# A low-rank product transposed on three row tiles instead of one, with its second operand loaded three times

## The chip, the cores and the metric

The kernel runs on one core of a Trainium2 chip. The metric is the device time of one execution in microseconds (us); lower is better. Engines are named as in the profile: PE is TensorE (PEld its weight loads), DVE is VectorE, ACT is ScalarE, POOL is GpSimd, SP is SyncE. DMA transfers are issued by SP and ACT ("hardware" queues) or by POOL ("software" queue) and carried out by 16 DMA engines of the core.

## What is computed

`x` is 8 x 4224 x 192 in float32. A causal convolution along the 4224 positions, with 7 taps and one set of softmax weights for each of 8 heads of 24 channels, gives y. Then a mixer follows:

```
xt = y.transpose(0, 2, 1)
h  = xt @ U @ V                      # U: 4224 x 32, V: 32 x 4224
u  = y + h.transpose(0, 2, 1)
out = u + np.maximum(u @ w_ch1, 0.0) @ w_ch2    # 192 -> 768 -> 192
```

So for each batch there is a small 32 x 192 product tt = U^T y over all positions, and h at a position is the matching column of V times tt.

## The kernel before, in words

**Tiles and groups.** The 8 x 4224 positions are cut into 264 tiles of 128 positions (33 for each batch), and 8 tiles make a group; there are 33 groups, `g` = 0 to 32. In a group the 8 tiles are numbered by a half `hf` (0 or 1) and `i` (0 to 3). The 192 channels are three blocks `c` of 64.

**Stages of a group.** `conv` or `conv32` make y of a batch as matmuls with banded matrices, `tt_mm`, `tt_split` and `tt_sum` make tt of a batch. `h_group` (L457 matmul, L479 addition on DVE) makes u, and `transp` (L498) transposes u by a DMA of SP's queue into `uT`, with positions along the columns and 64 channels of each half on 64 partitions. `w1` (L554 matmul, L568 and L570 ReLU on ACT and DVE) is the first layer from uT, `w2` (L583 matmul, L592 addition on DVE, L600 store) the second layer. The order is written out by hand: SLOTS lists which groups' first and second layers come when, and what lies between them. Every engine runs its own instructions in program order; semaphores make it wait for others.

**Groups 0 and 1 are special.** To start the first layer early, their u is not made first and then transposed. `yT_part` (L509) transposes y into PSUM by matmuls with the identity matrix, and `hT_part` (L524) adds the transposed h to the same PSUM bank: it multiplies 64 columns (block c) of tt with a stretch of V. ACT and DVE then copy the bank into `uT` (L256, L258 within `evac`). tt of batch 0 (`ttb[0]`, a tile of 128 partitions) is made with the matrix R4, which sums the four parts of 32 partitions and writes the sum four times, so that all four blocks of 32 partitions hold the same tt. `V0_sb` holds the first 2048 columns of V for these two groups. The rows of V and tt are 32, so a matmul of hT_part uses 32 of PE's 128 rows; `tile_position` names the row and the column at which it lies. The two halves hf lie on columns 0 and 64.

**Order at the start on PE:** convolution of batch 0 in pieces, tt (L402, L741, and L682 for the last piece, which reads `U4_sb`), yT_part(0), hT_part(0) with 10 matmuls, the rest of yT_part(1), hT_part(1) with 6 matmuls, w1(0), h_group(2), w1(1).

**POOL's order at the start:** x of batch 0 (two loads), U (two), x of batch 0 (two more), V0_sb (L133), W1_sb in four pieces (L137), zeroing and first piece of x of batch 1 (L74, L79), a copy that makes U4_sb (L701), V_sb in four quarters and a rest (L715, L722; read by L457 from h_group(2) on), W2_sb (L726), three more pieces of x of batch 1 (L79), copies for band2 (L759), and then x of the next batch. POOL's loads take turns on eight semaphores, so that one waits until the eighth before it has landed.

The lines of hT_part that the change touches are these:

```
lhsT=ttb[0][0:R, HB * c : HB * c + HB],
rhs=V0_sb[:, t0 + i0 * P : t0 + i1 * P],
tile_position=(0, HB * hf),
```

with R = 32, HB = 64 and P = 128.

Of the kernel before, what the change touches and what calls it, by code (L numbers as in the profile page):

```python
# [9 lines left out]
BF16 = mybir.dt.bfloat16  # L10
# [4 lines left out]
def kernel(  # L15
# [10 lines left out]
    nc = tc.nc  # L26
    P = nc.NUM_PARTITIONS
# [3 lines left out]
    R = moe_U.shape[1]  # L31
# [4 lines left out]
    GT = 8  # L36
# [3 lines left out]
    HB = P // 2  # L40
# [4 lines left out]
    cst = ctx.enter_context(tc.tile_pool(name="cst", bufs=1))  # L45
# [57 lines left out]
    def iota(t, pattern, base, mul):  # L103
# [20 lines left out]
        out=Ur[:, 0:nfull, :], in_=U4[0 : nfull * P, :].rearrange("(k p) c -> p k c", p=P)  # L124
# [4 lines left out]
        x_piece(k)  # L129


    V0_sb = cst.tile([R, 2 * GT * P], BF16, name="V0_sb")
    nc.gpsimd.dma_start(out=V0_sb[:], in_=moe_V[:, 0 : 2 * GT * P])  # L133
    W1_sb = cst.tile([P, 3, M4], BF16, name="W1_sb")
    for m0, m1 in ((0, 2 * P), (2 * P, M4)):
        for hf in range(2):
            nc.gpsimd.dma_start(  # L137
                out=W1_sb[HB * hf : HB * hf + HB, :, m0:m1],
                in_=moe_w_ch1[:, m0:m1].rearrange("(c k) m -> k c m", k=HB),
# [27 lines left out]
    for hh in range(2):  # L167
# [3 lines left out]
        out=dif[:], in0=dif[:], scalar1=rq[:, 0:1], scalar2=None, op0=ALU.add  # L171
# [5 lines left out]
        out=d_sb[:],  # L177
# [8 lines left out]
        out=hot[:],  # L186
# [6 lines left out]
        out=ident[:], in0=fp[:], scalar1=float(P), scalar2=None, op0=ALU.is_equal  # L193
# [9 lines left out]
        out=c_sb[:].rearrange("p k h -> p h k"),  # L203
# [5 lines left out]
    for hh in range(2):  # L209
# [3 lines left out]
            out=pr[:],  # L213
# [8 lines left out]
        out=Eq[:], in0=efp[:], scalar1=rq[:, 1:2], scalar2=None, op0=ALU.is_equal  # L222
# [3 lines left out]
        out=fp[:], in0=fp[:], scalar1=R - 1, scalar2=None, op0=ALU.bitwise_and  # L226
# [3 lines left out]
        out=R4[:], in0=fp[:], scalar1=0.0, scalar2=None, op0=ALU.is_equal  # L230
# [23 lines left out]
    def evac(eng, out, in_):  # L254
        if eng == "A":
            nc.scalar.activation(out=out, in_=in_, func=ACT.Copy)  # L256
        else:
            nc.vector.tensor_copy(out=out, in_=in_)  # L258
# [135 lines left out]
    ttb = [[] for _ in range(B)]  # L394
# [123 lines left out]
    def hT_part(g, parts):  # L518

        uTt[g] = uts.tile([P, 4, 3, P], BF16, name="uT")  # L520
        for c, i0, i1, p, _ in parts:
            for hf in range(2):
                t0 = (2 * g + hf) * 4 * P
                nc.tensor.matmul(  # L524
                    out=p[HB * hf : HB * hf + HB, 0 : (i1 - i0) * P],
                    lhsT=ttb[0][0:R, HB * c : HB * c + HB],
                    rhs=V0_sb[:, t0 + i0 * P : t0 + i1 * P],
                    start=False,
                    stop=True,
                    tile_position=(0, HB * hf),  # L530
                )
        for c, i0, i1, p, eng in parts:
            evac(
                eng,
                uTt[g][:, i0:i1, c, :],
                p[:, 0 : (i1 - i0) * P].rearrange("p (i t) -> p i t", t=P),
            )
# [161 lines left out]
    for r, (k0, k1) in KP[2].items():  # L699
        j = NB0 // 2 * r + k0  # L700
        nc.gpsimd.tensor_copy(  # L701
            out=U4_sb[:, o : o + k1 - k0, :, :],
            in_=U_sb[:]
# [9 lines left out]
    for q in range(4):  # L713
        src = moe_V[:, 0 : full * 8 * P].rearrange("r (k q t) -> r k q t", q=4, t=2 * P)
        nc.gpsimd.dma_start(  # L715
            out=V_sb[32 * q : 32 * q + 32, 0 : 2 * full, :].rearrange(
                "r (k a) t -> r k (a t)", a=2
            ),
            in_=src[:, :, q, :],
# [3 lines left out]
        out=V_sb[0:32, 2 * (NT // 8), :], in_=moe_V[:, (NT - 1) * P : NT * P]  # L723
# [23 lines left out]
    yT_part(1, parts1)  # L747
    tt_done(0, ps0)
    hT_part(0, parts0 + more)
    rest = [(c, 0, 4, bank(), "ADA"[c]) for c in (1, 2)]  # L750
    yT_part(1, rest)
    hT_part(1, parts1 + rest)
    band2 = cst.tile([P, H, QB], BF16, name="band2")
    for xp in XP[1:]:
        x_part(1, *xp)
    for r in range(4):
        q = slice(QB * r, QB * r + QB)
        for hh in range(2):
            nc.gpsimd.tensor_copy(  # L759
                out=band2[q, HQ * hh : HQ * hh + HQ, :],  # L760
                in_=bands[hh][q, :, HB * (r % 2) : HB * (r % 2) + QB],
# [86 lines left out]
```

## Time and profile before

| | |
|---|---|
| time, median of 3 runs | 324.98 us (324.97 to 325.1) |
| span of the profiled execution, first to last instruction | 323.2 us |
| PE busy | 317.6 us (98%) |
| DVE, ACT, POOL busy | 268.6, 170.0, 142.7 us |
| granted clock of PE | 1.000 |
| L524 (hT_part) | 16 matmuls, 18.34 to 20.5 us |
| L133 (V0_sb) | 1 load of 128 KB, issued at 7.23 us, landed 7.9 us later |
| L715 (V_sb) | 4 loads of 64 KB, issued from 14.04 us on |

For the profiled execution the page gives the span; the runs' time is 1.8 us above it, and no other time of that execution is given. Times within the profile are counted from the span's start. Busy time of PE includes matmuls that lie side by side once only, and the end of each is modelled. A load's landing is counted from the start of its issue on POOL.

### The profile page before, as it was taken

To read this page: it belongs to the slowest core of one execution; us is meant where nothing else is said; L and a number is where in the kernel's file an instruction comes from. 1 tells how busy PE (TensorE), PEld (TensorE's weight loads), DVE (VectorE), ACT (ScalarE), POOL (GpSimd) and SP (SyncE) were. 2 spreads that over 40 slices of the span, in tenths; PEclk is the share of its full clock that TensorE was granted. 3 is DMA by queue.
4 is the path that set the end of the run, shared out by engine and by line. 5 is a ranking of instruction groups with operands and counts; after the bars stand their busy time and mean duration, and the time that the engine had idled before them with its cause. 6 is when DMAs were issued, how large, how long until landed. Compare 5 with 4: busy or idle time off the path is not lost.

```text
span 323.2 us, 9583 instructions
## 1 busy us (share of the span) xinstructions
PE 317.6 (98%) x3996; PEld 223.7 (69%) x3996; DVE 268.6 (83%) x551; ACT 170.0 (53%) x344; POOL 142.7 (44%) x111
## 2 busy tenths in 40 slices
PE   8999999999999999999999999999999999999995
PEld 3747676478677647866864884687797497487495
DVE  6769989987977986997898699789888897896863
ACT  1766724860874397088239609824903902912910
POOL 8764179728957983992897497000000000000000
PEclk9999999999999999999999999999999999999999
DMA  9999993999998999599499957138268059048035
GB/s 106 192 191 183 206 209 100 196 192 257 208 135 200 246 142 190 166 189 209 130 237 192 181 149 194 52 105 231 61 178 262 3 150 275 18 121 271 2 121 173
DMA packets 122906, 53.51 MB, mean 166 GB/s; under 512 B 87760, under 2 KB 122832, under 8 KB 122864
## 3 DMA queue, kind: packets, MB, share of 16 engines
q1 hardware_dynamic: 84528, 38.08, 45.4%
q0 software_dynamic: 38192, 14.73, 39.2%
q8 instruction: 31, 0.51, 0.7%
q10 hardware_dynamic: 144, 0.10, 0.1%
q14 instruction: 11, 0.09, 0.1%
HBM read 29.49 MB, written 25.95 MB: 172 GB/s over the span
## 4 chain that ended last, share of the span: by engine, by line
PE 92%; ACT 3%; DMA 2%; DVE 1%; issue 0%; POOL 0%; POOLq 0%
PE ps L583 42%; PE ps L554 39%; PE ps L339 3%; PE ps L457 3%; DMA x_sb<-in_x_dram 2%; PE ps L402 2%; ACT rl_sb L568 2%; PE ps L369 1%; ACT y_sb L256 1%; PE ps L509 1%; DVE u_sb L479 1%; DVE rl_sb L570 1%; PE ps L524 0%; PE ps L428 0%; POOL x_sb L79 0%
## 5 line engine op out<-in xcount | busy, mean ns | idle before, releaser
L568 ACT ACTIVATE rl_sb<-ps 128x512 bf16<-128x512 f32 x233 | 124.3, 604 | 108.0 <-PE ps L554 96.0
L583 PE MATMUL ps<-W_sb,rl_sb 128*128 128x192 bf16 x1584 | 141.2, 246 | 0.2
L583 PEld LDWEIGHTS <-rl_sb 128*128 128x128 bf16 x1584 | 128.3, 98 | 11.8 <-issue 11.5
L554 PE MATMUL ps<-uT,W_sb 64*128 64x512 bf16 x1188 | 131.7, 376 | 0.0
L570 DVE TENSOR_SCALAR rl_sb<-ps 128x512 bf16<-128x512 f32 x163 | 105.3, 688 | 15.7 <-PE ps L554 15.4
L554 PEld LDWEIGHTS <-W_sb 64*128 64x128 bf16 x1188 | 66.9, 94 | 60.4 <-issue 3.9
L592 DVE TENSOR_TENSOR out_sb<-ps,u_sb 128x384 f32<-128x384 f32 (+1 forms) x133 | 70.4, 551 | 25.5 <-PE ps L583 25.0
L305 POOL COPY xb_sb<-x_sb 32x3072 bf16<-32x3072 bf16 (+1 forms) x24 | 67.4, 2824 | 0.5
L479 DVE TENSOR_TENSOR u_sb<-y_sb,ps 128x192 bf16<-128x192 bf16 (+1 forms) x168 | 66.3, 461 | 0.0
L293 POOL COPY xb_sb<-x_sb 128x3072 bf16<-128x3072 bf16 x12 | 32.7, 2742 | 42.1 <-PE ps L339 32.2
L256 ACT ACTIVATE y_sb<-ps 128x384 bf16<-128x384 f32 (+4 forms) x90 | 38.3, 520 | 9.7 <-PE ps L339 7.4
L79 POOL DMA_DIRECT2D x_sb<-in_x_dram x32 | 27.0, 848 | 9.6 <-PE ps L457 3.8
L258 DVE CAST y_sb<-ps 128x408 bf16<-128x408 f32 (+4 forms) x36 | 19.1, 578 | 1.3 <-PE ps L369 1.0
L457 PE MATMUL ps<-tt_sb,V_sb 32*128 32x192 bf16 x264 | 12.4, 246 | 0.1
L339 PE MATMUL ps<-x_sb,band 64*32 64x384 bf16 x192 | 12.1, 333 | 0.0
L339 PE MATMUL ps<-xb_sb,band 64*32 64x384 bf16 x192 | 12.1, 332 | 0.0
L457 PEld LDWEIGHTS <-V_sb 32*128 32x128 bf16 x264 | 4.7, 92 | 7.3 <-issue 7.3
L416 ACT ACTIVATE tt_hi<-ps 128x192 bf16<-128x192 f32 x8 | 2.6, 330 | 11.9 <-PE ps L402 11.9
L369 PE MATMUL ps<-x_sb,band 64*64 64x240 bf16 (+3 forms) x192 | 8.0, 276 | 0.2 <-DMA x_sb<-in_x_dram 0.2
L339 PEld LDWEIGHTS <-band 64*32 64x32 bf16 x384 | 4.5, 89 | 5.2 <-issue 2.4
L153 PE MATMUL ps<-zz 128*128 128x512 f32 (+1 forms) x10 | 6.7, 816 | 1.1 <-DVE zz L143 1.1
L369 PEld LDWEIGHTS <-band 64*64 64x64 bf16 x192 | 6.0, 106 | 2.1 <-issue 1.4
(65 smaller groups left out, 71.3 us busy)
## 6 DMA issues: line engine op xcount, KB each, us to landing
out_dram<-out_sb SPq DMA_DIRECT2D x131, 192.0 KB, 2.7
x_sb<-in_x_dram POOLq DMA_DIRECT2D x14, 384.0 KB, 6.9
x_sb<-in_x_dram POOLq DMA_DIRECT2D x7, 432.0 KB, 6.7
x_sb<-in_x_dram POOLq DMA_DIRECT2D x7, 408.0 KB, 8.0
x_sb<-in_x_dram POOLq DMA_DIRECT2D x1, 504.0 KB, 7.3
uT<-u_sb SPq DMA_TRANSPOSE x31, 3.5
x_sb<-in_x_dram POOLq DMA_DIRECT2D x1, 480.0 KB, 5.6
W_sb<-in_moe_w_ch_dram POOLq DMA_DIRECT2D x2, 192.0 KB, 7.8
```

Source lines behind the costliest of these rows:

```text
L79: return nc.gpsimd.dma_start(out=xt[b][HB * r : HB * r + HB, s0:s1, :], in_=x[b, blk * HB : (blk + s1 - s0) * HB, :].rearrange("(j p) d -> ...
L256: nc.scalar.activation(out=out, in_=in_, func=ACT.Copy)
L293: nc.gpsimd.tensor_copy(out=xbt[b][:, s0:s1, :], in_=xt[b][:, s0 + 1 : s1 + 1, :])
L305: nc.gpsimd.tensor_copy(out=xbt[b][q, s0:s1, :], in_=xt[b][q, s0:s1, :])
L339: nc.tensor.matmul(out=pp[r][QB * cg : QB * cg + QB, 0 : nk[r] * GS], lhsT=w[hr], rhs=t[hr, st : st + 2 * nk[r] - 1 : 2, hs], start=True, ...
L457: nc.tensor.matmul(out=banks[pr][:, a * D : (a + 1) * D], lhsT=V_sb[32 * q : 32 * q + 32, (j // 8) * 2 + j % 2, :], rhs=ttb[b][32 * q : 32 ...
L479: nc.vector.tensor_tensor(out=u_group(g)[:, i : i + n, :, hf, :], in0=yt[b][:, run[0] : run[0] + n, :].rearrange("p n (c k) -> p n c k", c=3),
L554: last = nc.tensor.matmul(out=pps[m][hf][:], lhsT=W1_sb[HB * hf : HB * hf + HB, c, m * P : (m + 1) * P], rhs=uTt[g][HB * hf : HB * hf + HB ...
L568: nc.scalar.activation(out=rl[:, m, hf, :], in_=pp[hf][:], func=ACT.Relu)
L570: nc.vector.tensor_scalar_max(out=rl[:, m, hf, :], in0=pp[hf][:], scalar1=0.0)
L583: last = nc.tensor.matmul(out=cps[:, a * D : (a + 1) * D], lhsT=rlt[g][:, m, hf, (i + a) * P : (i + a + 1) * P], rhs=W2_sb[:, m, :], start ...
L592: nc.vector.tensor_tensor(out=o[:, 0:n, :].rearrange("p n (c k) -> p n c k", c=3), in0=cps[:, 0 : n * D].rearrange("p (n c k) -> p n c k", ...
```

## The change

V0_sb gets 96 partitions instead of 32, and the same part of V is loaded three times by POOL, to partitions 0, 32 and 64. In hT_part, block c of the channels uses the rows 32c to 32c + 31 of tt's tile and of V0_sb, and the matmul lies on those rows of PE. The numbers, sizes and order of the matmuls stay as they are. On POOL's queue there are two more loads, ahead of W1's; what follows waits for landings that lie two loads further on. Line numbers from L134 on move by one.

```diff
-    V0_sb = cst.tile([R, 2 * GT * P], BF16, name="V0_sb")
-    nc.gpsimd.dma_start(out=V0_sb[:], in_=moe_V[:, 0 : 2 * GT * P])
+    V0_sb = cst.tile([3 * R, 2 * GT * P], BF16, name="V0_sb")
+    for c in range(3):
+        nc.gpsimd.dma_start(out=V0_sb[R * c : R * c + R, :], in_=moe_V[:, 0 : 2 * GT * P])
...
-                    lhsT=ttb[0][0:R, HB * c : HB * c + HB],
-                    rhs=V0_sb[:, t0 + i0 * P : t0 + i1 * P],
+                    lhsT=ttb[0][R * c : R * c + R, HB * c : HB * c + HB],
+                    rhs=V0_sb[R * c : R * c + R, t0 + i0 * P : t0 + i1 * P],
...
-                    tile_position=(0, HB * hf),
+                    tile_position=(R * c, HB * hf),
```

## The prediction

> **What bounds the kernel now.** I read the page first: busy times and the chain that ended last.
>
> ```profile
> PE 317.6 (98%) x3996; PEld 223.7 (69%) x3996; DVE 268.6 (83%) x551; ACT 170.0 (53%) x344; POOL 142.7 (44%) x111
> PE 92%; ACT 3%; DMA 2%; DVE 1%; issue 0%; POOL 0%; POOLq 0%
> ```
>
> The end is set by TensorE (PE) nearly everywhere, so time that PE saves is kept unless a wait takes it back. Second, the chain in order of time, from the stage that the change touches to the first layer of group 1:
>
> ```profile
> 17.89 0.46 PE ps L509 x12
> 18.35 0.83 PE ps L524 x10
> 19.18 0.57 PE ps L509 x16
> 19.75 0.76 PE ps L524 x6
> 20.51 1.23 PE ps L554 x10
> 21.74 3.04 ACT rl_sb L568 x6
> 24.79 0.04 issue
> 24.83 4.16 PE ps L554 x36
> ```
>
> The 16 matmuls of L524 (hT_part) hold 0.83 + 0.76 = 1.59 us of the path. Behind them stand the first layer of group 0 (L554), then ACT's emptying of its banks, to 24.8. Third, the timelines of PE and POOL:
>
> ```profile
> 18.34 0.84 PE L524 MATMUL ps<-V_sb,tt_sb 32*64 32x256 bf16 x10
> 19.11 0.64 PE L509 MATMUL ps<-ident,y_sb 128*64 128x128 bf16 x16
> 19.68 0.83 PE L524 MATMUL ps<-V_sb,tt_sb 32*64 32x512 bf16 x6
> 24.44 0.34 PE L457 MATMUL ps<-tt_sb,V_sb 32*128 32x192 bf16 x8
> ```
>
> ```profile
> 11.38 0.63 POOL L137 DMA_DIRECT2D W_sb<-in_moe_w_ch_dram  x1 [0.88 <-DMA Ur<-in_moe_U_dram]
> 12.12 0.84 POOL L79 DMA_DIRECT2D x_sb<-in_x_dram  x1
> 13.27 0.82 POOL L701 COPY U_sb<-U_sb 128x768 bf16<-128x768 bf16 x1 [0.31 <-ACT U_sb L256]
> 14.04 2.43 POOL L715 DMA_DIRECT2D V_sb<-in_moe_V_dram  x4
> 17.75 0.51 POOL L722 DMA_DIRECT2D V_sb<-in_moe_V_dram  x1 [1.27 <-DMA W_sb<-in_moe_w_ch_dram]
> ```
>
> PE leaves L524 0.77 us after it began, both times (18.34 to 19.11, 19.68 to 20.45). POOL issues loads and waits for older ones to land: a load may go out when the eighth before it has landed.
>
> **What the change removes: row tiles in turn.** Narrow windows of L524 show the starts of the pairs (the two halves hf run side by side): 18.34, 18.48, 18.59, 18.80, 18.91, then 19.68, 19.92, 20.12. A pair with 256 columns holds its rows for 0.11 us, one with 512 for 0.21, in turn, since all lie on rows 0 to 31. Now c = 0, 1, 2 get rows of their own. That such tiles run together is in the L457 row: 8 matmuls of 192 columns on four row tiles take 0.34 us from first start to last end, with 246 ns for each, so 0.34 - 0.25 = 0.09 for all 8 starts: four at a time.
>
> Group 0: c0 18.34, c0 again 18.48, c1 and c2 beside it at 18.48, c2 again 18.59. The last to stop streaming is c1, at 18.48 + 0.21 = 18.69, instead of 18.91 + 0.11 = 19.02. PE went on 0.09 after that (19.11), so now at 18.78: 0.33 less. Group 1: all three pairs at once, 0.21 instead of 20.12 + 0.21 - 19.68 = 0.65: 0.44 less. Sum 0.77. Bounds: nothing (row tiles still in turn) and 0.9 (the starts of L457 pace everything). I take 0.75, the two matmul rows being the nearest.
>
> The Trainium skill, TensorE: Matmul & The Clock Gate, Part 3 (Measured speedup vs the span model), gives 3.07 times for four row tiles of 512 columns. Three tiles would by that gain 2.3 times, my estimate from the page, and the sum would be about 0.65.
>
> **What is late next.** ACT and DVE empty group 0's banks: ACT from 18.68 for 1.09 us without a gap, DVE from 18.79 for 1.02 us. Neither gets faster: c1 is there at 19.81 at the latest. The first layer, now from 19.70, needs ACT's last bank at its second pair (19.70 + 0.21 = 19.91) and c1 at its third (20.12): no wait. Group 1's banks are emptied by ACT after 19.80 for 1.08 us, to 20.88; the first layer's first bank is ready at 21.73 - 0.75 = 20.98. So ACT and its 3 us block move forward whole.
>
> **What it adds: two loads on POOL, in front of 13 others.** V0 is issued at 7.23, takes POOL 0.56 and is landed 7.9 later, at 15.13. The x piece before it lands at 6.50 + 8.0 = 14.50, the first W1 piece after it at 7.75 + 7.9 = 15.65. The queue is one long line, so V0's share is 0.63 us. By the bytes (128 KB) at the rate of the nearest windows, 263 and 162 GB/s at 13.5 to 14.0 and 14.0 to 14.5, it is 0.50 to 0.81. Two more: 1.0 to 1.6; I take 1.3, from the landings.
>
> The Trainium skill, DMA: Bandwidth & Descriptors, Anatomy of one DMA, speaks against the change: about 2.0 us fixed for each such transfer and then its bytes, so two would be some 4.6 us if nothing overlapped; by that the sum ends about 2.3 us slower. The landings 0.5 to 0.6 apart say that the fixed part overlaps here.
>
> POOL's queue afterwards: V0 at 7.23, 7.75, 8.3; the four W1 pieces at 9.9 (waits for x, landed 9.59), 11.4 (U, 11.09), 12.0, 13.2 (x piece, 12.91), instead of 7.75, 8.40, 9.88, 11.38. x1's zeroing and first piece then wait for the x piece landed at 14.50: issue 14.8, where it was 12.12. Behind it stands the copy of U4 (L701): 15.6 to 16.45, was 13.27 to 14.09. Its reader, tt_late (L682), starts at 16.90: 0.4 us of cover left; each tenth beyond would be paid in full, since tt, L524 and all else hang on it. Then the V quarters from 16.5 to about 19 (14.04 to 16.47 before), V's rest, W2 (18.32, now about 19.7), three x1 pieces (from 19.20, now from 20.5) and the band2 copies (2.27 us, first needed at 68.97).
>
> Who needs them, with landings 1.3 later, PE 0.75 earlier: the first two W1 pieces 16.95 and 18.8 against 19.70; the others 19.4 and 20.2 against 20.98; W2 25.6 against 29.25 - 0.75 = 28.5; x1's last piece 32.2 against 37.0. All covered. Two of the copies of V0 land at 15.8 and 16.4 against 18.34. The tight one is V_sb for h2 (L457, 24.44): its last quarter landed at about 16.0 + 6.5 = 22.5, now 23.8 (23.5 to 24.1). PE would want it at 23.69; as h2's 8 matmuls take 0.1 to start and the next first layer is held by ACT until 24.83 - 0.75 = 24.08, about 0.2 is free. Cost 0 to 0.2, I take 0.03. Queues of SP and ACT are not moved; x2's pieces follow x1's and come at most 1.3 later, first for POOL's copies at 41.20, which end 9 us before their use at 68.97.
>
> **Sum.** -0.75 + 0.03 = -0.72 us. The page gives the profiled execution's span, 323.2 us; the runs' median, 324.98, lies 1.8 above it, and I leave that part as it is: span 322.5, time 324.26, 0.22% faster. A measurement of this kernel can tell about 0.2% (0.65 us) from no change, so this lies just outside.
>
> **Rivals.** (A) Part of the gain goes: tiles overlap less (0.65 or less), or V_sb is 0.2 or more past its cover. For it: both are within my bounds, and 0.07 us is all that separates 0.72 from the bound. Time 324.4 to 325.0. (B) Slower: V_sb's lateness decides. It takes over from a landing of about 23.9; the loss outweighs 0.75 from 24.65 on, and is over 0.2% from 25.3. That takes 1.4 us for each added copy, against 0.63 in the landings, or quarters whose landing follows their issue (now at about 18.4) by more than the 6.5 us of before: 18.4 + 6.5 = 24.9 gives a wait of 1.0 and 325.25, and 0.6 us more on POOL makes 325.8. Against it: the queue has its next load waiting at all times, and a later issue only shortens the wait in line. (C) The change doesn't do what it says: row tiles whose results leave by the same 64 columns run in turn, gain nothing, and only V_sb's delay could be paid (it is covered then, 23.8 against 24.44): 325.0, no change. Against it: L457's four row tiles share all 128 columns.
>
> **How the numbers follow.** Forecast (0.65 us or more gained) 0.55; A and C together 0.28 (A 0.22, C 0.06); B 0.17. The range: 323.95 (0.9 from the tiles, and a little more where evacuation follows) to 325.6, which takes in A, C and the covered edge of B and leaves out about 0.02 below and 0.17 above. Forecast alone: 323.95 to 324.33.
>
> **What would show it.** Right: L524 leaves PE after about 0.44 and 0.33 us instead of 0.77 twice; the first layer starts near 19.7, ACT's block near 21.0; the last V quarter lands near 23.8 and h2 stands near 23.8 in the timeline with hardly an idle gap named V_sb; then every later line 0.7 earlier. Wrong: pairs of L524 still 0.2 apart; L682 waiting for POOL; an idle gap of PE before L457 released by a DMA; or a V quarter landing after 24.

## The result, and the profile after

The changed kernel takes 327.0 us (median of 15 runs, 325.93 to 332.19), the kernel before beside it 325.1 us (15 runs, 324.9 to 326.84). The run of 332.19 us, at a granted clock of 0.990, is a slow execution and not in the ratio; the median of the other 14 is 326.95 us (to 329.9). The ratio is 1.0062, 95% interval 1.0038 to 1.0086: slower by about 1.9 us, where 0.7 us less was forecast. The profiled execution took 328.25 us (span 326.5), 1.25 us above the median. It is read first; two more profiles nearer to the median follow.

The page of the changed kernel (busy times; the granted clock in 40 slices; the chain that ended last, by engine):

```profile
PE 318.3 (98%) x3996; PEld 222.6 (68%) x3996; DVE 268.7 (82%) x551; ACT 169.9 (52%) x344; POOL 144.0 (44%) x113
...
PEclk9999799999999999999999999999999999999999
...
PE 86%; DMA 7%; POOL 2%; ACT 2%; DVE 1%; issue 0%; POOLq 0%
```

DMA's share of the chain has gone from 2% to 7%, and the fifth slice (about 33 to 41 us) has a lower clock. Lines after L133 are numbered one higher than before: L524 is L525, L554 is L555, L498 is L499.

The timeline of PE, the lines that answer to those of the prediction:

```profile
18.14 0.42 PE L525 MATMUL ps<-V_sb,tt_sb 32*64 32x256 bf16 x10
18.49 0.64 PE L510 MATMUL ps<-ident,y_sb 128*64 128x128 bf16 x16
19.06 0.41 PE L525 MATMUL ps<-V_sb,tt_sb 32*64 32x512 bf16 x6
19.41 4.06 PE L555 MATMUL ps<-uT,W_sb 64*128 64x512 bf16 x36
23.40 1.00 PE L458 MATMUL ps<-tt_sb,V_sb 32*128 32x192 bf16 x8
```

The row tiles do what they were to do. PE leaves L525 after 0.35 us both times (18.14 to 18.49, 19.06 to 19.41) instead of 0.77: 0.84 us saved. The first layer starts at 19.41, 1.04 us earlier than before (0.2 of that was there already at 18.14: in the profile of before, PE stood still for 0.18 us ahead of the last matmul of tt, L682). The last line is the first sign of trouble: h of group 2 takes 1.00 us instead of 0.34.

The chain of waits in order of time (start, duration, what), first of the changed kernel, then one line of the kernel before:

```profile
18.38 5.64 DMA V_sb<-in_moe_V_dram
24.02 0.05 issue
24.07 0.33 PE ps L458 x5
24.40 1.94 PE ps L555 x17
26.34 9.01 DMA uT<-u_sb
35.34 0.05 issue
35.39 3.76 PE ps L555 x18
39.15 2.61 ACT rl_sb L569 x5
```

```profile
33.83 2.09 PE ps L554 x18
```

The last quarter of V lands at 24.02; after it the lead over the kernel before is 0.5 us. Then the transposing DMA of group 2's u, which was in no chain before, takes 9.0 us and ends at 35.34. The same 18 matmuls that began at 33.83 now begin at 35.39, 1.56 us later, and take 3.76 us instead of 2.09, which is 1.67 more. Together 3.23 of the 3.3 us by which the two spans differ. From there to the end the two kernels run alike: each hundredth matmul after the 500th starts 3.3 us later.

The issue of that DMA on SP's queue, before and after:

```profile
27.14 1.52 SPq L498 DMA_TRANSPOSE uT<-u_sb  x1
```

```profile
26.34 2.66 SPq L499 DMA_TRANSPOSE uT<-u_sb  x1
```

It is issued 0.8 us earlier and lands 3.1 us later: 5.1 us after its issue before (at 32.2, 1.6 us ahead of its use), 9.0 us now. The windows of 1 us show what the DMA engines did (the last columns: granted clock, DMA share, GB/s), before:

```profile
30.00:31.00 1.00, 0.98 (x17) 0.69 (x16) 1.00 (x3) 0.18 (x1) 1.00 (x3) 1.00 0.48 90
31.00:32.00 1.00, 1.00 (x15) 1.00 (x13) 1.00 (x4) 0.00 (x0) 0.77 (x1) 1.00 1.34 249
```

and after:

```profile
31.00:32.00 1.00, 1.00 (x15) 1.00 (x13) 1.00 (x4) 0.00 (x0) 0.21 (x1) 1.00 0.95 94
32.00:33.00 1.00, 1.00 (x15) 1.00 (x13) 1.00 (x3) 0.00 (x0) 0.85 (x1) 1.00 2.62 92
33.00:34.00 1.00, 0.28 (x4) 0.05 (x1) 1.00 (x3) 0.00 (x0) 0.03 (x1) 1.00 0.13 8
34.00:35.00 1.00, 0.00 (x0) 0.00 (x0) 0.72 (x2) 0.00 (x0) 0.00 (x0) 1.00 1.22 212
...
36.00:37.00 1.00, 1.00 (x8) 0.38 (x6) 0.38 (x1) 0.42 (x1) 0.00 (x0) 0.50 1.60 188
```

In both there is a stretch in which little moves: about 1 us at 90 GB/s before, 3 us at 94, 92 and 8 GB/s after. The packets of SP's queue in the trace begin at 29.0 before and only at 30.2 after, when the line of software loads (POOL's queue) is nearly dry, and end at 31.7 and 34.7. The packets from 29.0 to 30.0 by queue (packets, MB, share of 16 engines; q1 is SP's, q0 the software queue), before:

```profile
q1 hardware_dynamic: 435, 0.11, 175.3%
q0 software_dynamic: 124, 0.04, 37.2%
```

and after, where SP's queue has none yet:

```profile
q0 software_dynamic: 480, 0.18, 155.4%
```

The 1568 packets of this DMA are the same in both, so the 3.1 us have two parts: the packets start 1.3 us later, and they take 4.5 us instead of 2.7, which is 1.7 more. The DMA issued at 49.45 before, with no software load about ("in clear air" below), has its first packet 1.2 us after the issue and is through them in 1.5 us.

PE stands still meanwhile (0.28, then 0.00 busy), and when it starts again the granted clock is 0.50 for 3 us: the 1.67 us.

### The profile page after: what moved, and what is told of

Its sections match the earlier page's. It is cut to its first block, busy times and chain, and to the rows that moved or that the text cites. A ratio compares the mean times of both kernels' runs of the same rounds, so it can differ in the third digit from the quotient of the medians.

```text
span 326.5 us, 9585 instructions
## 1 busy us (share of the span) xinstructions
PE 318.3 (98%) x3996; PEld 222.6 (68%) x3996; DVE 268.7 (82%) x551; ACT 169.9 (52%) x344; POOL 144.0 (44%) x113
## 4 chain that ended last, share of the span: by engine, by line
PE 86%; DMA 7%; POOL 2%; ACT 2%; DVE 1%; issue 0%; POOLq 0%
PE ps L584 40%; PE ps L555 38%; DMA V_sb<-in_moe_V_dram 5%; PE ps L340 3%; DMA uT<-u_sb 3%; PE ps L458 3%; PE ps L403 2%; POOL x_sb L79 1%; ACT y_sb L257 1%; ACT rl_sb L569 1%; DVE u_sb L480 1%; DVE rl_sb L571 1%; PE ps L429 0%; POOL V_sb L716 0%; DVE out_sb L593 0%
## 5 line engine op out<-in xcount | busy, mean ns | idle before, releaser
L555 PE MATMUL ps<-uT,W_sb 64*128 64x512 bf16 x1188 | 133.3, 380 | 2.1 <-DMA uT<-u_sb 2.1
L555 PEld LDWEIGHTS <-W_sb 64*128 64x128 bf16 x1188 | 66.3, 95 | 64.5 <-issue 5.7
L294 POOL COPY xb_sb<-x_sb 128x3072 bf16<-128x3072 bf16 x12 | 32.7, 2742 | 45.8 <-PE ps L340 32.9
L403 PE MATMUL ps<-y_sb,U_sb 128*32 128x192 bf16 x258 | 7.4, 247 | 0.0
```

What stands on the lines that cost most here:

```text
L294: nc.gpsimd.tensor_copy(out=xbt[b][:, s0:s1, :], in_=xt[b][:, s0 + 1 : s1 + 1, :])
L555: last = nc.tensor.matmul(out=pps[m][hf][:], lhsT=W1_sb[HB * hf : HB * hf + HB, c, m * P : (m + 1) * P], rhs=uTt[g][HB * hf : HB * hf + HB ...
```

## The experiments

All ran beside the kernel before, whose medians were 325.06 to 325.18 us. "Lead" is how much earlier PE starts its n-th matmul than in the profile of before, "landing" how long after its issue a transposing DMA is done.

### Each half alone

**Row tiles alone.** V0 is loaded once, and the rows that c = 1 and 2 read are zeroed, so their h in groups 0 and 1 is left out. Against the kernel before (shortened):

```diff
-    V0_sb = cst.tile([R, 2 * GT * P], BF16, name="V0_sb")
-    nc.gpsimd.dma_start(out=V0_sb[:], in_=moe_V[:, 0 : 2 * GT * P])
+    V0_sb = cst.tile([P, 2 * GT * P], BF16, name="V0_sb")
+    nc.gpsimd.dma_start(out=V0_sb[0:R, :], in_=moe_V[:, 0 : 2 * GT * P])
...
+    nc.vector.memzero(V0_sb[HB:P, :])
...
+            rc = (0, 64, 96)[c]        # rows of lhsT, rhs and tile_position
```

> Three row tiles without the two added loads: V0 is loaded once, to partitions 0 to 31; the blocks c = 1 and 2 lie on partitions 64 and 96, which are zeroed by DVE early on, so their h in groups 0 and 1 is left out; the count and sizes of the matmuls are those of the changed kernel. Theory LINE (the transposing DMA of group 2's u gets the DMA engines only when the line of software loads runs dry; the added loads lengthen the line): PE passes its first layer of group 0 at about 19.4 as in the changed kernel, the line ends as before, the transposed u of group 2 lands at 32.2 or earlier, no wait of PE for it, time about 324.0 (1.0 below before). Theory EARLY (PE's lead alone makes the next batch's loads go out earlier and collide with the transposing DMA): u of group 2 lands near 35 here too, PE waits some 2 us for it, time 326 or more.

Measured: 325.99 us (324.0 to 328.21, 10 runs), ratio 1.0016, 0.9985 to 1.0048; profiled span 324.0. **Loads alone.** V0 is loaded three times, the matmuls stay on rows 0 to 31. Against the changed kernel (shortened), as all cuts below unless they say otherwise:

```diff
-                    lhsT=ttb[0][R * c : R * c + R, HB * c : HB * c + HB],
+                    lhsT=ttb[0][0:R, HB * c : HB * c + HB],   # rhs, tile_position alike
```

> The two added loads alone: V0 is loaded three times, but all matmuls use rows 0 to 31 as before. LINE: PE's start stays as before (first layer of group 0 at about 20.4), the line of software loads ends 1.3 us later, the transposed u of group 2 lands 1.3 to 3 us later than 32.2, PE (which wants it at 33.8) waits 0 to 1.5 us, time 325 to 327. EARLY: no lead, no collision, time as before, 325.0.

Measured: 325.91 us (325.14 to 327.35, 10 runs), ratio 1.0016, 0.9992 to 1.0041. Its timeline of PE:

```profile
34.60 2.77 PE L555 MATMUL ps<-uT,W_sb 64*128 64x512 bf16 x24 [0.98 <-DMA uT<-u_sb]
```

The loads alone make the wait: group 2's DMA lands 7.6 us after its issue, PE waits, and at the 500th matmul it is 0.84 us behind. The tiles alone do not: the landing is 6.6, the DMA is there at 32.9 and PE needs it at 33.0; the lead of 0.75 us is kept up to 76 us. But it does not reach the end. The chain of the row tiles alone, later:

```profile
69.52 8.75 DMA out_dram<-out_sb
78.27 0.03 issue
```

```profile
DVE out_sb L594 <- DMA out_dram<-out_sb: 2.1, 1, 2.1
```

DVE waits 2.1 us for an output buffer whose store came late. At 66.6 the transposing DMA of group 7 was issued among loads of batch 3's x; it landed 11.3 us later (8.3 before), and 1.76 us of PE's time went between 77 and 87 us. So two things are seen: the added loads bring the first wait, and a lead by itself runs into a second meeting of a transposing DMA with software loads. Each is read from one profile. By the medians neither half alone is told from the kernel before, since both intervals take in 1; the two differences, 0.9 and 0.8 us, add up to about what the whole change lost.

### Which loads

**x2's first two loads held back** until the second layer of group 0 has begun.

```diff
-    LOADS = {2: [(1, 5), (1, 5)], 3: ...}
+    LOADS = {3: ...}
-  1: ["h3", "l2:2"]
+  1: ["h3", "l2:0", "l2:1", "l2:2"]
```

> The changed kernel whole, but the first two loads of batch 2's x are held until the first two tiles of the second layer of group 0 are done (issue about 30.5 and 31.3 instead of 28.7 and 29.5). LINE, with the collision as its second half: the transposing DMA has the engines to itself once batch 1's last load has landed, u of group 2 lands at about 33 instead of 35.3, PE waits about 0.3 us instead of 2.1, time 324.3 to 325. If the added loads' delay alone counted and not the collision, it would still land near 35 and the time would stay at 326 to 327.

Measured: 327.43 us (326.12 to 329.39, 8 runs), ratio 1.0067, 1.0033 to 1.01; landing 9.6 us, the wait 2.7. My expectation for it was wrong. SP's packets start at 30.5 us here, as in the changed kernel, though x2's loads go out only at 30.4 and 31.2, so x2's loads are not what makes that start late; they were still waiting while the packets ran, so the sluggish flow behind the start is not cleared of them.

**The last piece of x1 held back** until group 1's first layer is at its fourth block. This takes from the end of the line what the change had put in at its head.

```diff
-    for xp in XP[1:]:
+    for xp in XP[1:3]:
...
+            if g == 1:
+                held(x_part(1, *XP[3]), ends[3])
```

> The changed kernel whole, with the added loads, but the last load of batch 1's x (408 KB) is held until the fourth block of group 1's first layer is done (issue about 27 instead of 23.5), so that the line of software loads runs dry some 2 us earlier, at about 28. LINE: the transposing DMA of group 2's u starts to flow at about 28 and lands at 31 to 32.5 instead of 35.3, PE has no wait for it at 32.7 and keeps its lead of about 1 us to 65 us; time 324.1 to 325 unless a later transposing DMA collides in the same way (that of group 7, issued at about 66 among batch 3's loads). The rival of this round, STRAGGLER (the transposing DMA is slow by itself when issued at that moment, whatever stands in line): it still takes 8 us or more, PE waits, 326 to 327.

Measured: profiled at 325.98 us, the fastest of its 9 runs (to 328.6, median 327.77), ratio 1.006, 1.0032 to 1.0087. Group 2's DMA now lands 5.9 us after its issue and PE does not wait for it. The held load goes out at 27.4 instead of 23.5 us, behind that DMA. But the chain now has the next one:

```profile
40.41 7.49 DMA uT<-u_sb
71.55 7.24 DMA out_dram<-out_sb
```

PE waits 1.4 us for group 3 (landing 7.5, 5.6 before). In this one profile shortening the line cures the first wait, which supports the length of the line as its cause, but the kernel as a whole is no faster than the changed one; that the load moved back makes the next one is likely, but no run separates it.

**One added load instead of two,** with c = 2 on rows 0 to 31 again: two row tiles.

```diff
-    for c in range(3):
+    for c in range(2):
...
+            rc = (0, R, 0)[c]
```

> The changed kernel with one added load instead of two (V0 on rows 0-31 and 32-63; c = 2 reads rows 0-31 again, so two row tiles run at once and the third layer's set follows; the result is whole). Theory (the line of software loads holds the transposing DMA of group 2, which gets through when that line runs dry): the line is longer by about 0.65 us, so this DMA lands between the 32.2 us of the kernel before and the 35.3 us of the changed one, about 33.5, and PE waits for it 0 to 1.2 us; lead at 32 us about 0.5; time 325.3 to 326.3. Rival (the second added load, or something that only three row tiles do, makes the wait): landing by 32.5 and no wait, time at most 324.9; or the wait is the same 2.1 us and more as with two.

Measured: landing 6.8 us, PE's wait 0.3 (0.6 at the weight load), lead at the 500th matmul 0.34; here, and only here, a lead lasted to the end of a profile (span 322.9; with 324.7 us the fastest of its 10 runs). The median is 326.45 all the same (to 327.79), ratio 1.0026, 1.0000 to 1.0051. The dose fits: with no, one and two added loads group 2's DMA lands 5.1 to 6.6, 6.8, and 7.6 to 9.6 us after its issue where x1's pieces go out as before. The traces show it more cleanly in the first packet of that DMA: at 28.9 to 29.3 us with no added load, whether it was issued at 26.3 or at 27.2; at 29.6 with one; at 30.2 to 30.5 with two; and at 27.6 to 28.4 in the three runs that hold the last piece of x1 back. From there its packets take 2.7 to 3.0, 3.2 and 3.6 to 4.8 us, and 3.6 to 6.1 where the piece is held.

### How much was the wait, how much the clock

**The changed kernel, profiled twice more.** Both had the same expectation:

> The changed kernel itself, for a second profile: the profiled execution took 328.25 us where the median was 327.0. Theory: in an execution nearer to the median the transposing DMA of group 2 also lands late, 7 to 9.5 us after its issue, with a wait of 1 to 2.3 us on PE and a lower clock behind it. Rival (the late landing belongs to the one profiled execution, and the median is high for another reason): landing by 6.5 us, no wait at the first layer of group 2, and the loss at other places.

> The changed kernel itself, for a third profile; the expectations are those of the second.

Measured: 327.07 and 326.68 us, spans 325.3 and 324.9. The chain, waits and a window of the third profile:

```profile
26.30 9.14 DMA uT<-u_sb
35.49 4.06 PE ps L555 x36
```

```profile
PE ps L555 <- DMA uT<-u_sb: 2.3, 1, 2.3
```

```profile
36.00:37.00 1.00, 1.00 (x12) 0.42 (x10) 0.62 (x1) 0.61 (x2) 0.00 (x0) 1.00 1.59 194
```

The late landing belongs to every profile (9.0, 9.3, 9.1 us), the low clock only to the first. Of the 15 runs of the result three have a mean granted clock of 0.995 or less (328.21, 328.25 and 332.19 us), so most lose little or nothing by it; two others took 329.48 and 329.9 us at 1.000, and no profile shows why. Group 2 starts 1.66 us later than before in the third profile, whose span is 1.7 longer, and 1.97 in the second, 2.1 longer. That is the median's 1.9 us: a wait of 2.3 to 2.5 us less the lead of 0.5 to 0.6.

**The gap filled** with 20 matmuls on W1_sb whose results are overwritten.

```diff
                 pps[m] = [bank(), bank()]
+                for n in range(20 if g == 2 and m == 0 else 0):
+                    q = HB * (n % 2)
+                    nc.tensor.matmul(out=pps[m][n % 2][:], lhsT=W1_sb[q : q + HB, 0, 0:P],
+                        rhs=W1_sb[q : q + HB, 1, 0 : 4 * P], start=True, stop=True, ...)
```

> The changed kernel with 20 matmuls of 64x512 more on PE just before the first layer of group 2, on W1_sb alone (their results are overwritten by the next matmul's start): 10 pairs, about 2.3 us at full clock, in the place where PE stood still for 2.1 us. Theory (the changed kernel lost about 2.1 us by the late transposing DMA and another 1.7 us because the granted clock was 0.5 for some 3 us behind the still stretch): the landing of group 2's uT stays late (8 to 10 us after its issue), the granted clock stays at 1.00 at 33 to 40 us, PE's lead is at matmul 500 about 1.5 us better than in the changed kernel's profile (about 42 instead of 43.4 us), and the time is 0.5 to 1.8 us below the changed kernel's median: 325.3 to 326.5. Rival (the clock falls for another reason, or PE waits little in most executions): the clock is below 1 there in spite of the work, or the fill costs its 2.3 us: 327.5 or more.

Measured: 327.78 us (326.74 to 328.5, 4 runs), ratio 1.0069, 1.0045 to 1.0093. Its chain:

```profile
33.35 2.27 PE ps L556 x20
35.62 1.99 PE ps L565 x18
```

The clock stays at 1.00, but the group starts at 35.62, no earlier than in the changed kernel; the transposing DMA had landed at 34.9, so 0.7 us of that is the fill itself. This profile, the slowest of the four, loses 1.5 us more at 81 to 87 us. The rival's second form holds: the time is over 327.5, and in most executions there is no lost clock to win back.

### Without the loads: copies, and moves around the second meeting

**Copies by DVE and ACT** of V0 to rows 32 to 95; V0 loaded once.

```diff
     conv_piece(2)
+    H0 = GT * P
+    nc.vector.tensor_copy(out=V0_sb[R : 2 * R, :], in_=V0_sb[0:R, :])
+    nc.scalar.activation(out=V0_sb[2 * R : 3 * R, 0:H0], in_=V0_sb[0:R, 0:H0], func=ACT.Copy)
+    nc.vector.tensor_copy(out=V0_sb[2 * R : 3 * R, H0:], in_=V0_sb[0:R, H0:])
```

> The change without added loads and with the right result: V0 is loaded once, and DVE and ACT copy it from partitions 0 to 31 to 32 and 64 after their last evacuations of the convolution (DVE 2048 and 1024 columns, ACT 1024), at about 16.8. LINE: as the tiles alone, less whatever the copies delay tt's copy on DVE (17.7) or the first bank's copy on ACT (18.5): time 324.0 to 324.6. EARLY: 326 or more. A cost of the copies shows as a wait of L524's line for DVE or ACT after 18.1.

Measured: 326.17 us (325.4 to 329.39, 10 runs), ratio 1.0029, 1.0001 to 1.0058. Landing 6.1, a wait of at most 0.2, lead 0.75 up to 76 us, and lost as with the tiles alone:

```profile
70.49 8.07 DMA out_dram<-out_sb
```

Three runs tried to take the second meeting away. In the diff, "h7" is group 7's addition and its transposing DMA, moved seven places later (0 to 7; the expectation below says five); the first run also has the copies (the second of DVE's behind tt) and the held x1 piece, the second is the kernel before with both moves, the third has the copies and h7 alone.

```diff
-                0: ["h7"],
+                7: ["h7"],
```

> V0 loaded once and copied by DVE and ACT (the last copy now behind tt's copy on DVE), the last load of batch 1's x held as in the run before it, and u of group 7 made five places later in the second layer of groups 3 to 5 (p = 7 instead of 0), so that its transposing DMA is issued at about 75 us, when batch 3's loads have landed, instead of 66.6. LINE: neither transposing DMA meets the line; DVE has no wait for a store of out_sb near 78; the lead of the row tiles, 0.8 to 1.0 us, stays to the end: 324.0 to 324.3, with less spread than the changed kernel. STRAGGLER: group 2's still takes 6 to 9 us and the time is 325 or more.

Measured: 328.13 us (326.65 to 328.86, 4 runs), ratio 1.0094, 1.0061 to 1.0127. Group 7's DMA lands in 3.3 us, as wanted, but group 2's in 7.7, with a wait of 1.0 us.

> The kernel before, row tiles in turn and V0 on 32 rows, with only the two moves of order (last load of batch 1's x held, u of group 7 made later). LINE: no collision to avoid costs it time in its usual runs, so 325.0 as before, with fewer of the runs near 326 to 327. If the moves themselves brought the gain of the run before this one, it would be near 324 too; if they cost, 325.5 or more.

Measured: 327.37 us (325.55 to 328.76, 10 runs), ratio 1.0056, 1.0033 to 1.008: the moves cost the kernel before by themselves. Group 3's DMA lands in 7.8 us (a wait of 1.7), and later an x load that takes 11.1 us stands in the chain.

> V0 loaded once and copied by the engines, u of group 7 made later, but batch 1's last load not held. LINE: group 2's transposing DMA lands near 32.9, about when PE wants it (33.0): a wait of 0 to 0.6 us that varies from run to run; group 7's lands within 5 us and no store is late: 324.2 to 324.8. If the collision of group 7's DMA was not what took the lead of the engine-copy run, the time stays near 326.

Measured: 325.91 us (325.61 to 327.72, 9 runs; a tenth, at a granted clock of 0.992, took 330.51), ratio 1.0029, 1.0009 to 1.005. In the profile, the slowest of the nine, the lead is 0.87 up to the 500th matmul; then x loads of 14.1 and 11.4 us in the chain take it, and 1.8 us more.

In three runs the stores of groups 3, 4 and 5 left SP's queue, where they stand behind group 7's DMA: with the copies, in the kernel before, and with the row tiles alone.

```diff
-        eng = nc.scalar if t + n == NTT else nc.sync
+        eng = nc.scalar if t + n == NTT or g in (3, 4, 5) else nc.sync
```

> V0 loaded once and copied to rows 32-63 and 64-95 by DVE and ACT, three row tiles, and the output stores of groups 3, 4 and 5 issued on ACT's queue instead of SP's. Theory (in the copies' kernel the lead of 0.75 us was kept to 76 us and lost at 77 to 87 us because the stores stood on SP's queue behind the transposing DMA of group 7): the stores no longer wait for it, DVE's wait for a free out_sb goes, and the lead is kept beyond 87 us: time 324.2 to 324.8, faster than before. Rival (the stores are late because the DMA engines serve the line of batch 3's x loads and the transposing DMA in any case, whatever queue the stores come from): the wait for out_sb stays at 1 to 2 us, or ACT's own work is late behind its queued stores; time 325.5 to 326.5.

> The kernel before with the same stores of groups 3, 4 and 5 on ACT's queue, as a control for the run with copies. Both theories: without a lead there is no wait for out_sb to remove, so the time is that of before within 0.3 us, 324.8 to 325.4; if ACT is delayed by the issues, up to 326.

> Row tiles alone (V0 loaded once to rows 0-31, rows 64-127 zeroed, so that h of the second and third layer in groups 0 and 1 lacks the part that V0 gives), with the stores of groups 3, 4 and 5 on ACT's queue. Theory (behind a late transposing DMA on the same queue the stores came late): the lead of 0.75 is kept past 87 us and the time is 324.2 to 324.6. Rival (the stores are late whatever their queue): wait for out_sb of 1 to 2 us as in the row tiles alone, time 325.5 to 326.2.

Measured: 327.7 (326.81 to 329.36, 6 runs; ratio 1.0083, 1.0055 to 1.0111), 326.74 (326.64 to 327.0, 6 runs; 1.0041, 1.0026 to 1.0056) and 327.85 us (326.87 to 328.89, 4 runs; 1.0076, 1.0047 to 1.0105). The control's chain:

```profile
67.86 10.70 DMA out_dram<-out_sb
```

A store on ACT's queue, with no transposing DMA ahead of it there, takes 10.7 us: the stores are late whatever their queue. My theory of the order within SP's queue falls, and the control loses by the move itself (its interval lies above 1). None of these kernels beats the kernel before.

## Why the prediction was wrong, point by point

**Tiles: right.** Forecast 0.33 + 0.44 = 0.77, taken as 0.75; measured 0.42 + 0.42. The estimate from the Trainium skill's factor for four row tiles was 2.3 times; the row is 0.77 to 0.35, 2.2 times. Rival C falls; of rival A the second condition came (V_sb more than 0.2 past its cover), but not its time.

**POOL's order: right.** The U4 copy ran at 15.65 to 16.47 (forecast 15.6 to 16.45) and its reader did not wait. W1, W2 and x1's pieces kept their cover. x1's first three pieces landed 1.3 to 1.4 us later, as forecast; the last landed at 34.26 (32.86 in the third profile), not at 32.2, and x2's four pieces 2.3 to 5.0 us later, not "at most 1.3".

**V_sb: the mechanism right, the size too small.** The last quarter landed at 24.02, not 23.8; the wait took 0.5 us of the lead of 1.04, where 0.03 (at most 0.2) was taken. "A V quarter landing after 24" was among the signs of an error. Rival B, which needed 24.65 to lose, did not come about: the loss has another place. The 2.3 us slower that the prediction sets beside its sum, for loads that do not overlap, lies near the measured 1.9 by luck: by that working the quarter would have come 4.6 us later, and it came 1.6 later (22.40 to 24.02).

**The failed step** is a sentence: "Queues of SP and ACT are not moved; x2's pieces follow x1's and come at most 1.3 later". The instruction order on SP is indeed unmoved. But its transposing DMA shares the 16 DMA engines with POOL's line, and I priced the 1.3 us only for the loads in that line and their readers, not for a DMA of another queue that is in flight at its end. Its row was there before: issued at 27.14, landed 5.1 later, used at 33.83, 1.6 us of cover. The tiles' lead takes half of that cover, since PE needs the result 0.8 us earlier; in the tiles' own profile the landing was 0.7 us later as well, which left 0.1. With the loads alone the landing was 2.3 us later, with both 3.1. Of these 3.1 us the longer line explains the later start of the packets, 1.3; that they also ran 1.7 longer came with the added loads, but why is open. "Then every later line 0.7 earlier" failed for the same reason, and in a second way: with the tiles alone a lead got to 76 us and was lost to late stores. The 1.9 us lost lie outside my range because no rival had this mechanism.

**Turns of the queues, and the clock.** The trace shows SP's packets starting 3.9 us after the issue, with POOL's line nearly dry, where 1.2 us is enough in clear air. The Trainium skill, DMA: Bandwidth & Descriptors, Queues, rings and completion order, says that each DMA engine goes round between the queues that have work, a packet at a time; by that the transposing DMA would have had its share from the start, and the prediction could have left it out. These runs do not agree with so even a share, as far as SP's queue had work all that time, which is not shown: the issue's own row lasts 2.66 us here against 1.40 in clear air, so part of the delay may lie ahead of the queue. On the clock: in the four profiles with the longest gaps at this place PE stood still 2.1, 2.7, 2.5 and 2.3 us, and the clock fell to 0.50 for about 3 us after the first two (the changed kernel's first profile, and x2 held back). The Trainium skill, TensorE: Matmul & The Clock Gate, Why this matters for your kernels, asks for no gap above some 3 us; here 2.1 was enough once and 2.5 was not.

**What stays open.** Why the DMA engines almost stop for up to 1 us (8 GB/s, share 0.13) with a transposing DMA in flight is not settled; the length of the software line says when this stretch comes, not how long it lasts. It is also not the only condition: with copies, no added load and a piece of x1 held back, group 2's DMA still took 7.7 us; its packets started early, at 27.6, and all but two of the 1568 had started by 31.7, but the last two only at 33.6. And whether some order keeps the tiles' gain to the end was not found: one profile of one added load kept 0.3 us, and the median of these runs did not.

## What to carry to other kernels

When a change lengthens a line of loads, or lets the bottleneck run ahead, look up every transfer in flight at the end of that line, on any queue, and write down its landing, its use and the cover between them; here 1.6 us of cover on a DMA that stood in no chain decided the sign. A gain early in a program is kept only if each later meeting of loads and stores with their readers has cover for it. Take a second profile before pricing what the first shows: the lost clock of 1.7 us was in one profile of three.

## What the runs showed of the hardware that was not expected

A transposing DMA of SP's queue lands 3.2 to 3.3 us after its issue where no software load moves (issued at 49.45 and 55.27 us before) and 4.7 to 14.1 us after it among software loads (4.7 for group 3 of the changed kernel, 14.1 for group 7 with the row tiles alone and stores on ACT's queue). While both are in flight the rate can fall to 8 GB/s for 1 us, where 170 to 250 is usual around it. Its first packet came 1.2 us after the issue in clear air, and 1.3 to 4.1 us after it for group 2, the later the more of the software line lay ahead. Three row tiles beside two column tiles ran at once: the six matmuls of 512 columns took 0.35 us until PE went on, the same as the ten of 256.
